# Attention backward for one query row per head: scores as 512-column matmuls in four column groups, spread by one-hot fp32 matmuls

## The chip, the core and the metric

The kernel runs on one core of one Trainium2 chip. The metric is the device time of one execution in microseconds, and the time of a kernel is the median over several executions. A core has a matrix engine (PE, TensorE, with its weight loads listed apart as PEld), a vector engine (DVE), a scalar engine (ACT), a general engine (POOL) and a queue engine (SP). POOL and SP issue the transfers here, and all transfers run on the core's 16 DMA engines.

## The reference

For each of 2 x 32 = 64 heads there is one query row q (128 values), a K and a V of 8192 rows of 128 bf16 values, and a gradient row `grad_out`. The kernel computes the output and the gradients to q, K and V:

```python
scores = jnp.einsum("bhqd,bhkd->bhqk", q, k) * scale     # one row of 8192 a head
p = _softmax(scores, axis=-1)
out = jnp.einsum("bhqk,bhkd->bhqd", p, v)
_out, _vjp = jax.vjp(_f, q, k, v)
_grads = _vjp(grad_out)
```

Written out for a head: s = K q, p = softmax(s x scale), o = p V; dp = V g with g the row of `grad_out`; ds = p (dp - sum(p dp)) x scale; dq = ds K, dK = ds outer q, dV = p outer g. K and V are read once (268 MB together) and dK and dV, of the same size, are written once.

## The kernel before

**Data.** A head's K and its V are tiles of [128 partitions, 64 rows, 128 columns] in bf16, 2 MB each: partition p holds the 64 rows 64p to 64p+63. Twelve such tiles (`NTILE`) are in SBUF, so six heads are under way. A tile is loaded by SP, read by the matrix engine, and then overwritten in place with dK or dV, and stored from there by POOL. The load for the head six later waits for that store (`load`, line 98; `outer`, line 412). In eight heads (`SPREAD`) the dK store is cut in 126 and 2 partitions.

**Chunks and steps.** A tile is worked in four chunks (`NCH`) of 16 rows (`CH`), so a head has eight chunks, first K's, then V's. The loop at line 423 runs over chunks of all heads, and one turn of it is called a step here. The order of all instructions is written out by hand and pinned (`pin`), so each engine works its instructions in just that order. A step holds work of several heads, chosen by r, the step counted from the head's first one. `transpose_chunk` is at r = 0 to 7: 16 transposes of 128 x 128 into PSUM, and one ACT copy of 128 x 2048 to SBUF (`ev`). `score_chunk` follows one step later. `acc` is at r = 8 to 11 for V (o) and 12 to 15 for K (dq). `outer` is at r = 9 to 12 for dV and 13 to 16 for dK. Since a head starts every eight steps, each step has one `transpose_chunk`, one `score_chunk`, one `acc` and one `outer`.

**Scores.** `score_chunk` issues 16 matmuls. Each takes one transposed 128 x 128 block as its weights and the head's q (or g) as its only moving column, so that each gives one column of s or dp, laid out as [128 partitions, 64].

**Sums for o and dq.** `acc` issues four matmuls of 512 moving columns (four rows of the tile side by side). The weights are 64 columns (`CW`) of `E_pad` or `dS_pad`, and the results go to two groups (`NG`) of 64 partitions of one PSUM bank by turns. Only four of the 64 rows of each group's result are wanted, each in one of its four 128-column blocks; `pick` takes them with the mask `diag` (four DVE instructions of 128 x 128), and `join` adds over the partitions by a matmul with ones.

**PSUM.** The transposes have two buffers of two banks, `acc` two banks, the tile `sw` (s, and room for the softmax maximum) one, and `dpw` (dp, the sums, and `qbp`, the broadcast of q or g) one: eight in all.

**The softmax of a head.** `max_part` at r = 4, `max_all` at r = 5, `max_spread` and `expo` at r = 6, `normalise_p` at r = 7, `weigh` at r = 8, `normalise_ds` at r = 9. `broadcast` makes q and g ready in all partitions for `outer`.

Of the kernel before, what the change touches and what calls it, by code (L numbers as in the profile page):

```python
# [11 lines left out]
BF16 = mybir.dt.bfloat16  # L12
F32 = mybir.dt.float32

CH = 16
QT = 4
CW = 64
NG = 2
NTILE = 12
FIRST = 6  # L20
SPREAD = range(4, 60, 7)
# [3 lines left out]
def kernel(  # L25
# [11 lines left out]
    nc = tc.nc  # L37
    B, H, Sq, D = q.shape
    Sk = k.shape[2]
    P = nc.NUM_PARTITIONS  # L40
    assert Sq == 1 and D == P
    BH = B * H
    assert BH <= P
    NT = Sk // P
    assert NT * P == Sk and NT % CH == 0
    NCH = NT // CH
    SL = 2 * NCH
# [4 lines left out]
    pin = tc.keep_in_program_order  # L52

    const = ctx.enter_context(tc.tile_pool(name="const", bufs=1))
    kvp = ctx.enter_context(tc.tile_pool(name="kv", bufs=1))
    evp = ctx.enter_context(tc.tile_pool(name="ev", bufs=2))
    work = ctx.enter_context(tc.tile_pool(name="work", bufs=1))
    small = ctx.enter_context(tc.tile_pool(name="small", bufs=2))
    ps_tp = ctx.enter_context(tc.tile_pool(name="ps_tp", bufs=2, space=bass.MemoryType.PSUM))
    ps_sdp = ctx.enter_context(tc.tile_pool(name="ps_sdp", bufs=1, space=bass.MemoryType.PSUM))  # L60
# [15 lines left out]
    heads = [Head() for _ in range(BH)]  # L76
# [13 lines left out]
    def load(i, w, pieces=(NCH,)):  # L90
        h = heads[i]
        t = kvp.tile([P, NT, D], BF16, tag=f"kv{slot_of(i, w)}", name="kvt")
        h.tile[w] = t
        src = (v_v if w else k_v)[i]
        c = 0
        for m in pieces:
            n0, n1 = c * CH, (c + m) * CH
            pin(load_eng.dma_start(out=t[:, n0:n1, :], in_=src[:, n0:n1, :]))  # L98
            c += m
# [4 lines left out]
    for w, a in enumerate((q, grad_out)):  # L104
        rows = a.rearrange("b h s d -> (b h s) d")
        r0 = FIRST if w == 0 else 0
        if r0:
# [3 lines left out]
                    out=qd_nat[:r0, w, :], in_=rows[:r0], max_dma_last_dim=D  # L111
# [11 lines left out]
    ident_f = const.tile([P, P], F32)  # L123
    masks.make_identity(nc, ident_f[:])
    ones = const.tile([P, 1], F32)
    nc.vector.memset(ones[:], 1.0)
    groups = [g * P // NG for g in range(NG)]
    diag = const.tile([P, QT], F32)
    nc.vector.memset(diag[:], 0.0)
    for g in groups:  # L130
        nc.vector.tensor_copy(out=diag[g : g + CW], in_=ident_f[g : g + CW, g : g + QT])

    NW = NT + CW - QT
    E_pad = const.tile([P, NW], BF16)
# [1 line left out]
    nc.vector.memset(E_pad[:], 0.0)  # L136
    nc.vector.memset(dS_pad[:], 0.0)

    qdT = const.tile([P, 2, BH], BF16)
    for w in range(2):  # L140
        tps = ps_m.tile([P, BH], BF16, tag=f"acc{w}", name="tps")
        nc.tensor.transpose(tps[:], qd_nat[:BH, w, :], ident_bf[:BH, :BH])
        nc.vector.tensor_copy(out=qdT[:, w, :], in_=tps[:])

    dqT = const.tile([P, BH], BF16)
    oT = const.tile([P, BH], BF16)

    def begin_s(i):

        h = heads[i]  # L150
        sw = ps_sdp.tile([P, NT + P + 1], F32, tag="s", name="sw")
        h.s = sw[:, 0:NT]
        h.mT = sw[0:1, NT : NT + P]
        h.mb = sw[:, NT + P :]

    def begin_dp(i):

        h = heads[i]
        dpw = ps_sdp.tile([P, NT + 2 + D], F32, tag="dp", name="dpw")
        h.dp = dpw[:, 0:NT]  # L160
        h.lsum = dpw[:, NT : NT + 2]
        h.qbp = dpw[:, NT + 2 :]

    def broadcast(i, w):

        h = heads[i]
        pin(
            nc.tensor.matmul(  # L168
                h.qbp,
                lhsT=qdT[:, w, i : i + 1].to_broadcast([P, P]),  # L170
                rhs=ident_bf[:],
                start=True,
                stop=True,
            )
        )
        h.qb[w] = small.tile([P, D], BF16, tag=f"qb{w}", name="qb")
        pin(nc.vector.tensor_copy(out=h.qb[w][:], in_=h.qbp))  # L177

    def transpose_chunk(i, c):
        w, c = divmod(c, NCH)  # L180
        src = heads[i].tile[w]
        tp = ps_tp.tile([P, CH, P], BF16, tag="tp", name="tp")
        for t in range(CH):
            pin(nc.tensor.transpose(tp[:, t, :], src[:, c * CH + t, :], ident_bf[:]))  # L184
        ev = evp.tile([P, CH, P], BF16, tag="ev", name="ev")
        pin(nc.scalar.copy(out=ev[:], in_=tp[:]))  # L186
        return ev

    def score_chunk(i, c, ev):
        h = heads[i]  # L190
        w, c = divmod(c, NCH)
        dst = h.dp if w else h.s
        for t in range(CH):
            pin(
                nc.tensor.matmul(  # L195
                    dst[:, c * CH + t : c * CH + t + 1],
                    lhsT=ev[:, t, :],
                    rhs=qdT[:, w, i : i + 1],
                    start=True,
                    stop=True,  # L200
                )
            )

    def max_part(i):
        h = heads[i]
        h.mp = small.tile([P, 1], F32, tag="mp", name="mp")
        pin(nc.vector.reduce_max(out=h.mp[:], in_=h.s, axis=AX.X))  # L207
# [120 lines left out]
    def acc(i, w, c):  # L328
# [6 lines left out]
        for m in range(CH // QT):  # L335
            n0 = c * CH + m * QT
            g = groups[m % NG]
            pin(
                nc.tensor.matmul(  # L339
                    h.acc[w][g : g + CW, :],  # L340
                    lhsT=wts[:, n0 : n0 + CW],
                    rhs=rows[:, n0 : n0 + QT, :].rearrange("p n d -> p (n d)"),
                    start=(c == 0 and m < NG),
                    stop=(c == NCH - 1 and m >= CH // QT - NG),
                )
# [42 lines left out]
    def outer(i, w, c, ends):  # L388

        h = heads[i]  # L390
        n0 = c * CH
        shape = [P, CH, D // 2, 2]
        pin(
            nc.vector.tensor_tensor(  # L394
                out=h.tile[w][:, n0 : n0 + CH, :].rearrange("p n (e t) -> p n e t", t=2),
                in0=h.qb[w][:]
                .rearrange("p (e t) -> p e t", t=2)
                .unsqueeze(1)
                .to_broadcast(shape),
                in1=h.pair[w][:, n0 : n0 + CH, :].unsqueeze(2).to_broadcast(shape),  # L400
                op=ALU.mult,
            )
        )
        if c + 1 in ends:
            at = ends.index(c + 1)
            b0, b1 = (ends[at - 1] if at else 0) * CH, (c + 1) * CH
            dst = (dv_v if w else dk_v)[i]
            if w == 0 and i in SPREAD:
                by_rows(store_eng, dst, h.tile[w], (P - 2, 2))
            else:  # L410
                eng = load_eng if len(ends) > 1 else store_eng
                pin(eng.dma_start(out=dst[:, b0:b1, :], in_=h.tile[w][:, b0:b1, :]))  # L412
# [10 lines left out]
    for g in range(SL * BH + O0 + NCH + 4 - SL):  # L423
        now = [(g // SL - b, g % SL + b * SL) for b in range(4)]
        now = [(i, r) for i, r in now if 0 <= i < BH]

        def at(r0):

            return next((i for i, r in now if r == r0), None)

        def within(r0):

            return next(((i, r - r0) for i, r in now if r0 <= r < r0 + NCH), None)

        if (i := at(O1 + NCH)) is not None and i + AHEAD < BH:
            load(i + AHEAD, 0)
        if (i := at(O0 + NCH)) is not None and i + AHEAD < BH:
            load(i + AHEAD, 1)
        if x := within(O1):
            outer(x[0], 1, x[1], last if x[0] == BH - 1 else whole)  # L440
        if x := within(O0):
            outer(x[0], 0, x[1], last if x[0] == BH - 1 else whole)
        ev = None
        if g < SL * BH:
            i, r = divmod(g, SL)
            if r == 0:
                begin_s(i)
            if r == 3:
                begin_dp(i)
                broadcast(i, 1)  # L450
            if r == 6:
                broadcast(i, 0)
            ev = transpose_chunk(i, r)
        if (i := at(A1 + NCH + 2)) is not None:
            join(i, 1)
        if (i := at(A0 + NCH + 2)) is not None:
            join(i, 0)
        if x := within(A1):
            acc(x[0], 1, x[1])
        if x := within(A0):  # L460
            acc(x[0], 0, x[1])
        if (i := at(NCH + 2)) is not None:
            max_spread(i)
            expo(i)
        if prev is not None:
            score_chunk(*prev)
        prev = (g // SL, g % SL, ev) if ev is not None else None

        if (i := at(NCH)) is not None:
            max_part(i)  # L470
        if (i := at(NCH + 1)) is not None:
            max_all(i)
        if (i := at(NCH + 3)) is not None:
            normalise_p(i)
        if (i := at(SL)) is not None:
            weigh(i)
        if (i := at(SL + 1)) is not None:
            normalise_ds(i)
        if (i := at(A1 + NCH)) is not None:
            pick(i, 1)  # L480
        if (i := at(A0 + NCH)) is not None:
            pick(i, 0)

    for w, (src, dst) in enumerate(((dqT, out_1), (oT, out_0))):
        tps = ps_m.tile([BH, P], BF16, tag=f"acc{w}", name="tps")
# [34 lines left out]
```

## Time and profile before

| what | before |
|---|---|
| median of 8 runs | 1285.68 us (1284.7 to 1289.62) |
| the profiled execution | 1285.78 us, its span 1284.0 us |
| bytes read from and written to HBM | 268.47 MB each |
| busy: PE / PEld / DVE / ACT | 88% / 67% / 73% / 76% |
| DMA queues, share of 16 engines | loads (SP) 49.9%, stores (POOL) 48.8%, instructions 0.7% |

The span is the time from the first to the last instruction of the profiled execution; 1.8 us lie outside it. A busy share is the time in which an engine had an instruction in work. It is an average over the span and doesn't tell what the end waits for. For the DMA engines the page gives, in 40 slices of 32 us, the mean busy share of the 16 engines and the rate in GB/s. The groups of instructions give a kind's count, its busy time in total (overlapping ones counted once), the mean duration of one in ns, and how long the engine stood idle just before them, with what ended the wait.

### The profile page before, as it was taken

What the parts mean: (1) busy time and instruction counts of PE and PEld (TensorE: products, weight loads), DVE (VectorE), ACT (ScalarE), POOL (GpSimd) and SP (SyncE); (2) the same over time, 40 slices, a digit from 0 to 9 for tenths busy, and PEclk for the clock granted to TensorE, in tenths of its full rate; (3) what the DMA queues carried; (4) which work ended last, traced back from release to release, by engine and by line L of the source; (5) the groups of instructions that cost most, each with busy time, mean ns of one, the idle gap of its engine ahead of it and who ended that gap; (6) DMA issues with size and microseconds to landing.
All of it is one profiled execution on the core that took longest, in us unless ns stands there. A gap on an engine that the chain in (4) does not pass through costs nothing.

```text
span 1284.0 us, 42576 instructions
## 1 busy us (share of the span) xinstructions
PE 1129.4 (88%) x19268; PEld 857.8 (67%) x19268; DVE 936.0 (73%) x2122; ACT 975.8 (76%) x641; POOL 76.1 (6%) x143
## 2 busy tenths in 40 slices
PE   6999999989988988898889798997989889889881
PEld 5777777667766766666667576675667667667660
DVE  2888888778777777677777677776778677777772
ACT  6888888878777877787777687886778678777760
POOL 0000000000000000000000000000000000000000
PEclk9999999999999999999999899998989899999895
DMA  9999999999999999999999999999999999999996
GB/s 387 425 427 426 427 426 428 426 428 426 427 428 425 415 428 428 427 420 428 428 427 422 422 429 427 425 426 426 427 426 426 425 427 427 426 424 427 426 410 256
DMA packets 40194, 539.68 MB, mean 420 GB/s; under 512 B 5196, under 2 KB 5196, under 8 KB 6476
## 3 DMA queue, kind: packets, MB, share of 16 engines
q1 hardware_dynamic: 20172, 272.70, 49.9%
q0 software_dynamic: 19840, 264.25, 48.8%
q8 instruction: 150, 2.46, 0.7%
q14 instruction: 32, 0.26, 0.0%
HBM read 268.47 MB, written 268.47 MB: 418 GB/s over the span
## 4 chain that ended last, share of the span: by engine, by line
DMA 31%; another core or an unknown queue 31%; PE 24%; DVE 10%; issue 1%; SPq 1%; ACT 1%; DVEq 0%; ACTq 0%
DMA kvt<-in_v_dram 24%; PE tp L184 10%; PE acc L339 6%; DMA kvt<-in_k_dram 6%; DVE kvt L394 6%; PE dpw L195 3%; PE sw L195 3%; DVE sel L362 2%; SPq L98 1%; ACT ev L186 1%; PE dpw L282 1%; DVE sel L356 1%; DMA qd_nat<-in_q_dram 1%; DVE mp L207 0%
## 5 line engine op out<-in xcount | busy, mean ns | idle before, releaser
L186 ACT COPY ev<-tp 128x2048 bf16<-128x2048 bf16 x512 | 954.9, 1866 | 268.4 <-PE tp L184 257.3
L184 PE MATMUL tp<-ident_bf,kvt 128*128 128x128 bf16 x8192 | 557.4, 223 | 97.3 <-DMA kvt<-in_v_dram 82.3
L394 DVE TENSOR_TENSOR kvt<-qb,pair 128x2048 bf16<-128x2048 bf16 x512 | 621.1, 1214 | 0.2
L184 PEld LDWEIGHTS <-kvt 128*128 128x128 bf16 x8192 | 488.2, 100 | 104.4 <-DMA kvt<-in_v_dram 86.4
L195 PEld LDWEIGHTS <-ev 128*128 128x128 bf16 x8192 | 242.9, 96 | 208.9 <-issue 152.1
L339 PE MATMUL acc<-kvt,dS_pad 128*64 128x512 bf16 x1024 | 169.2, 413 | 0.8 <-DVE dqT L379 0.8
L339 PE MATMUL acc<-kvt,E_pad 128*64 128x512 bf16 x1024 | 160.0, 393 | 0.0
L195 PE MATMUL dpw<-qdT,ev 128*128 128x1 bf16 x4096 | 140.7, 164 | 17.3 <-DVE qb L177 16.5
L362 DVE SCALAR_TENSOR_TENSOR sel<-acc,diag,sel 128x128 f32<-128x128 f32 x384 | 134.6, 351 | 13.6
L195 PE MATMUL sw<-qdT,ev 128*128 128x1 bf16 x4096 | 141.9, 164 | 1.1 <-ACT ev L186 1.1
L207 DVE TENSOR_REDUCE mp<-sw 128x1 f32<-128x64 f32 x64 | 14.4, 225 | 160.4 <-PE sw L195 160.4
L412 POOL DMA_DIRECT2D out_dram<-kvt x118 | 63.4, 537 | 1085.7 <-DVE kvt L394 867.6
L339 PEld LDWEIGHTS <-dS_pad 128*64 128x64 bf16 x1024 | 37.7, 111 | 24.8 <-issue 6.1
L247 DVE CAST E_pad<-E_f 128x64 bf16<-128x64 f32 x64 | 12.5, 195 | 55.8 <-ACT E_f L238 55.8
L339 PEld LDWEIGHTS <-E_pad 128*64 128x64 bf16 x1024 | 36.4, 108 | 21.2 <-issue 0.5
L376 PE MATMUL acc<-ones,sel 128*128 128x1 f32 x256 | 43.5, 239 | 6.2 <-DVE sel L362 6.2
L282 PE MATMUL dpw<-ld,ones 128*128 128x1 f32 x256 | 46.3, 250 | 0.1
L376 PEld LDWEIGHTS acc<-ones,sel 128*128 128x128 f32 x256 | 39.3, 194 | 7.3 <-DVE sel L362 7.3
L356 DVE TENSOR_SCALAR sel<-acc,diag 128x128 f32<-128x128 f32 x128 | 44.1, 345 | 0.0
L253 DVE CUSTOM_DVE_ANT_0 junk<-E_f,dpw 128x64 bf16<-128x64 f32 x64 | 14.1, 221 | 37.5 <-PE dpw L195 37.5
L177 DVE CAST qb<-dpw 128x128 bf16<-128x128 f32 x128 | 35.4, 277 | 6.0 <-PE dpw L168 6.0
L282 PEld LDWEIGHTS dpw<-ld,ones 128*128 128x128 f32 x256 | 38.2, 188 | 0.5 <-DVE ld L253 0.5
(44 smaller groups left out, 314.5 us busy)
## 6 DMA issues: line engine op xcount, KB each, us to landing
out_dram<-kvt POOLq DMA_DIRECT2D x118, 2048.0 KB, 67.8
kvt<-in_v_dram SPq DMA_DIRECT2D x64, 2048.0 KB, 19.8
kvt<-in_k_dram SPq DMA_DIRECT2D x63, 2048.0 KB, 19.9
out_dram<-kvt POOLq DMA_DIRECT2D x8, 2016.0 KB, 73.0
out_dram<-kvt SPq DMA_DIRECT2D x8, 512.0 KB, 22.7
kvt<-in_k_dram SPq DMA_DIRECT2D x2, 512.0 KB, 4.5
kvt<-in_k_dram SPq DMA_DIRECT2D x1, 1024.0 KB, 7.0
out_dram<-kvt POOLq DMA_DIRECT2D x8, 32.0 KB, 72.4
```

The source lines that it names most:

```text
L177: pin(nc.vector.tensor_copy(out=h.qb[w][:], in_=h.qbp))
L184: pin(nc.tensor.transpose(tp[:, t, :], src[:, c * CH + t, :], ident_bf[:]))
L186: pin(nc.scalar.copy(out=ev[:], in_=tp[:]))
L195: nc.tensor.matmul(dst[:, c * CH + t : c * CH + t + 1], lhsT=ev[:, t, :], rhs=qdT[:, w, i : i + 1], start=True, stop=True,)
L207: pin(nc.vector.reduce_max(out=h.mp[:], in_=h.s, axis=AX.X))
L282: nc.tensor.matmul(out, lhsT=ones[:].to_broadcast([P, P]), rhs=col, start=True, stop=True)
L339: nc.tensor.matmul(h.acc[w][g : g + CW, :], lhsT=wts[:, n0 : n0 + CW], rhs=rows[:, n0 : n0 + QT, :].rearrange("p n d -> p (n d)"), start=( ...
L356: nc.vector.tensor_scalar(out=h.sel[:], in0=block, scalar1=diag[:, 0:1], scalar2=None, op0=ALU.mult)
L362: nc.vector.scalar_tensor_tensor(out=h.sel[:], in0=block, scalar=diag[:, b : b + 1], in1=h.sel[:], op0=ALU.mult, op1=ALU.add,)
L376: nc.tensor.matmul(h.acc[w][:, 0:1], lhsT=h.sel[:], rhs=ones[:], start=True, stop=True)
L394: nc.vector.tensor_tensor(out=h.tile[w][:, n0 : n0 + CH, :].rearrange("p n (e t) -> p n e t", t=2), in0=h.qb[w][:] .rearrange("p (e t) -> ...
L412: pin(eng.dma_start(out=dst[:, b0:b1, :], in_=h.tile[w][:, b0:b1, :]))
```

## The change

The scores are made the other way round. The weights are now 32 columns around the head's q, and the moving operand is 512 columns of the transposed chunk. Four such matmuls, one for each group of 32 PSUM partitions, cover a chunk. In `qdT` the q of each head is put at every fourth column, with zeros between them, and the window `q0` is moved back by one column with each chunk. So q stands in the window's column c for chunk c, and chunk c's scores come out in row c of each group; all four chunks add into one bank (`raw`). The rows that belong to other heads' q are not picked.

`keep_raw` copies the bank [128, 512] to SBUF, in fp32, once a half head (K's four chunks, or V's). `spread_rows` then issues four fp32 matmuls, each with a 128 x 128 block of that copy as its weights and the one-hot table `sel4` (16 columns) as the moving operand. They pick the 16 wanted rows and lay the scores out as [128, 64] as before.

s, dp, the sums and `qbp` now share one PSUM tile of one bank (`begin`, at r = 4), and `raw` takes the bank that is left. The steps of the softmax move: `keep_raw` at r = 4 and 8, `spread_rows` at r = 5 and 9, `max_part` from 4 to 5, `max_all` from 5 to 6, `max_spread` and `expo` from 6 to 7, `normalise_p` from 7 to 8, `weigh` from 8 to 9, `normalise_ds` from 9 to 10, and `broadcast` from 3 to 4 for g (it is at 6 for q in both). `transpose_chunk`, `acc`, `outer`, `pick`, `join` and the loads and stores keep their steps. `acc` has the same four matmuls a step, now with 32 weight columns and in four groups of 32 partitions; `diag` and the width of `E_pad` and `dS_pad` follow.

```diff
-CW = 64
-NG = 2
+CW = 32
+NG = 4
+SG = 4
+SW = 32
...
+    sel4 = const.tile([P, NCH, SG], F32)
+    nc.vector.memset(sel4[:], 0.0)
+    for g in range(SG):
+        nc.vector.tensor_copy(
+            out=sel4[g * SW : (g + 1) * SW, :, g],
+            in_=ident_f[g * SW : (g + 1) * SW, g * SW : g * SW + NCH],
+        )
+
+    Q0 = NCH - 1
+    qdT = const.tile([P, 2, Q0 + NCH * BH + SW], BF16)
+    nc.vector.memset(qdT[:], 0.0)
...
+    def begin(i):
+
+        h = heads[i]
+        sw = ps_sdp.tile([P, 2 * NT + 2 * P + 4], F32, tag="s", name="sw")
+        h.score = (sw[:, 0:NT], sw[:, NT : 2 * NT])
+        h.s, h.dp = h.score
+        h.mT = sw[0:1, 2 * NT : 2 * NT + P]
+        h.qbp = sw[:, 2 * NT + P : 2 * NT + 2 * P]
+        h.lsum = sw[:, 2 * NT + 2 * P : 2 * NT + 2 * P + 2]
+        h.mb = sw[:, 2 * NT + 2 * P + 2 : 2 * NT + 2 * P + 3]
...
     def score_chunk(i, c, ev):
+
         h = heads[i]
         w, c = divmod(c, NCH)
-        dst = h.dp if w else h.s
-        for t in range(CH):
+        if c == 0:
+            h.raw = ps_sdp.tile([P, QT * P], F32, tag="raw", name="raw")
+        q0 = Q0 + NCH * i - c
+        for g in range(SG):
             pin(
                 nc.tensor.matmul(
-                    dst[:, c * CH + t : c * CH + t + 1],
-                    lhsT=ev[:, t, :],
-                    rhs=qdT[:, w, i : i + 1],
+                    h.raw[g * SW : (g + 1) * SW, :],
+                    lhsT=qdT[:, w, q0 : q0 + SW],
+                    rhs=ev[:, g * QT : (g + 1) * QT, :].rearrange("p n d -> p (n d)"),
+                    start=(c == 0),
+                    stop=(c == NCH - 1),
+                )
+            )
+
+    def keep_raw(i):
+
+        h = heads[i]
+        h.rows = work.tile([P, QT * P], F32, tag="rows", name="rows")
+        pin(nc.vector.tensor_copy(out=h.rows[:], in_=h.raw[:]))
+
+    def spread_rows(i, w):
+
+        h = heads[i]
+        for t in range(QT):
+            pin(
+                nc.tensor.matmul(
+                    h.score[w].rearrange("p (n t) -> p n t", t=QT)[:, :, t],
+                    lhsT=h.rows[:, t * P : (t + 1) * P],
+                    rhs=sel4[:].rearrange("p c g -> p (c g)"),
                     start=True,
                     stop=True,
                 )
...
-        if (i := at(NCH + 2)) is not None:
+        if (i := at(NCH + 1)) is not None:
+            spread_rows(i, 0)
+        if (i := at(SL + 1)) is not None:
+            spread_rows(i, 1)
+        if (i := at(NCH + 3)) is not None:
             max_spread(i)
             expo(i)
         if prev is not None:
@@ -467,14 +502,18 @@
         prev = (g // SL, g % SL, ev) if ev is not None else None
 
         if (i := at(NCH)) is not None:
+            keep_raw(i)
+        if (i := at(SL)) is not None:
+            keep_raw(i)
+        if (i := at(NCH + 1)) is not None:
             max_part(i)
-        if (i := at(NCH + 1)) is not None:
+        if (i := at(NCH + 2)) is not None:
             max_all(i)
-        if (i := at(NCH + 3)) is not None:
+        if (i := at(NCH + 4)) is not None:
             normalise_p(i)
-        if (i := at(SL)) is not None:
+        if (i := at(SL + 1)) is not None:
             weigh(i)
-        if (i := at(SL + 1)) is not None:
+        if (i := at(SL + 2)) is not None:
             normalise_ds(i)
```

More of the change, by code (lines that the diff above doesn't have):

```diff
@@ L137 @@
     nc.vector.memset(dS_pad[:], 0.0)
-    qdT = const.tile([P, 2, BH], BF16)
+    sel4 = const.tile([P, NCH, SG], F32)
[8 more added lines that the diff above has]
+    nc.vector.memset(qdT[:], 0.0)
     for w in range(2):
@@ L142 @@
         nc.tensor.transpose(tps[:], qd_nat[:BH, w, :], ident_bf[:BH, :BH])
-        nc.vector.tensor_copy(out=qdT[:, w, :], in_=tps[:])
+        nc.vector.tensor_copy(
+            out=qdT[:, w, Q0 : Q0 + NCH * BH].rearrange("p (i f) -> p i f", f=NCH)[:, :, 0],
+            in_=tps[:],
+        )
     dqT = const.tile([P, BH], BF16)
     oT = const.tile([P, BH], BF16)
-    def begin_s(i):
+    def begin(i):
         h = heads[i]
[L151 to L162, printed above, removed]
+        sw = ps_sdp.tile([P, 2 * NT + 2 * P + 4], F32, tag="s", name="sw")
[5 more added lines that the diff above has]
+        h.mb = sw[:, 2 * NT + 2 * P + 2 : 2 * NT + 2 * P + 3]
     def broadcast(i, w):
@@ L169, in broadcast @@
                 h.qbp,
-                lhsT=qdT[:, w, i : i + 1].to_broadcast([P, P]),
+                lhsT=qdT[:, w, Q0 + NCH * i : Q0 + NCH * i + 1].to_broadcast([P, P]),
                 rhs=ident_bf[:],
@@ L191, in score_chunk @@
         w, c = divmod(c, NCH)
-        dst = h.dp if w else h.s
-        for t in range(CH):
+        if c == 0:
+            h.raw = ps_sdp.tile([P, QT * P], F32, tag="raw", name="raw")
+        q0 = Q0 + NCH * i - c
+        for g in range(SG):
             pin(
                 nc.tensor.matmul(
-                    dst[:, c * CH + t : c * CH + t + 1],
-                    lhsT=ev[:, t, :],
-                    rhs=qdT[:, w, i : i + 1],
+                    h.raw[g * SW : (g + 1) * SW, :],
[4 more added lines that the diff above has]
+                )
+            )
+    def keep_raw(i):
[10 more added lines that the diff above has]
+                    rhs=sel4[:].rearrange("p c g -> p (c g)"),
                     start=True,
@@ L445 @@
             i, r = divmod(g, SL)
[L446 to L449, printed above, removed]
+            if r == NCH:
+                begin(i)
                 broadcast(i, 1)
-            if r == 6:
+            if r == NCH + 2:
                 broadcast(i, 0)
```

## The prediction

> **What bounds the kernel now.** I read the page first: engine shares, the DMA slices, the DMA queues.
>
> ```profile
> span 1284.0 us, 42576 instructions
> PE 1129.4 (88%) x19268; PEld 857.8 (67%) x19268; DVE 936.0 (73%) x2122; ACT 975.8 (76%) x641; POOL 76.1 (6%) x143
> ...
> DMA  9999999999999999999999999999999999999996
> GB/s 387 425 427 426 427 426 428 426 428 426 427 428 425 415 428 428 427 420 428 428 427 422 422 429 427 425 426 426 427 426 426 425 427 427 426 424 427 426 410 256
> ...
> q1 hardware_dynamic: 20172, 272.70, 49.9%
> q0 software_dynamic: 19840, 264.25, 48.8%
> q8 instruction: 150, 2.46, 0.7%
> ```
>
> PE looks tight at 88%, but the DMA engines are full in every slice but the last. So the question is whether PE or the DMA engines set the pace, and the waits answer it.
>
> ```profile
> PE tp L184 <- DMA kvt<-in_v_dram: 82.3, 45, 6.1
> PE dpw L195 <- DVE qb L177: 16.5, 51, 0.5
> ```
>
> PE waits 82 us for V loads, and SP's own waits are almost all for a store to free a tile (1139.6 us in 116 waits). Loads wait for stores, compute waits for loads: the DMA engines bound it. How much room has compute? A head moves 4 x 2.097 MB, which at 427 GB/s takes **19.6 us**. In the timeline near 200 us, where loads are still ahead, two stores of the same kind are issued at 200.27 and 217.59: compute needs **17.3 us** a head when nothing holds it up. So there are 2.3 us to spare in each head.
>
> Then the end, in the windows (us, busy time by engine, clock, DMA share, GB/s).
>
> ```profile
> 1180.00:1235.00 55.00, 48.87 (x811) 36.64 (x807) 40.90 (x92) 41.71 (x28) 2.97 (x6) 0.94 1.01 427
> 1240.00:1248.00 8.00, 6.38 (x94) 4.36 (x91) 6.57 (x18) 4.07 (x5) 0.53 (x1) 0.93 0.81 342
> 1248.00:1262.00 14.00, 7.56 (x31) 3.26 (x31) 12.63 (x24) 0.00 (x0) 0.00 (x0) 0.50 1.02 424
> 1264.00:1273.00 9.00, 0.00 (x0) 0.00 (x0) 0.00 (x0) 0.00 (x0) 0.00 (x0) 0.50 0.53 222
> 1273.00:1281.00 8.00, 0.00 (x0) 0.00 (x0) 0.00 (x0) 0.00 (x0) 0.00 (x0) 0.50 0.43 178
> ```
>
> The last compute ends at 1262; transfers go on for 19 us at a share of 0.53 and then 0.43, that is, on 8.5 and then 7 of 16 DMA engines, each at its usual pace (178 / 6.9 = 26 GB/s; 427 / 16 = 27 before). These seven are simply behind the others. As they were full up to 1240 and still have 19 us of work when the last store is given out, I take them to be busy from start to end. Then the end is **the bytes of the late DMA engines over their rate**, and compute may finish up to some 19 us later or any amount earlier without moving it.
>
> **What the Trainium skill says.** "TensorEngine Tiling (Array Packing)", Tiling Modes: 128x32 gives four tiles that work in parallel, and a change of mode drains the engine. The trace shows two tiles: the four `acc` matmuls of a step take 0.55 us, while "TensorE: Matmul & The Clock Gate" (Part 3) gives 2.38 times for three column tiles; no run here shows four yet. "PSUM — Partial Sum Buffer" (PSUM bank collisions): the compiler's scheduler adds a dependency between two engines on one bank and quadrant even where columns differ. The trace agrees: score matmuls waited 16.5 us for the copy of `qbp`, other columns of their bank. "Runtime: NRT & Kernel Launch" (Instruction fetch mechanics): instructions come by the sequencer's own DMA queue in blocks of 16 KiB, 256 instructions. It fits: 2 x 19,268 PE instructions / 256 = 150.5, and queue 8 has 150 packets.
>
> **The change part by part.** All is for one head unless said otherwise.
>
> *Matmuls of the scores.* Out: 128 with one column; a step's 16 take 0.42 us of PE's time (from their start to the next transposes, 216.97 to 217.39). In: 4 a step with 512 columns. Two rounds of two in `acc` take 0.55; a round less, at an estimated 0.216 (512 columns, TensorE page), is 0.34. Bounds: 0.34 if four overlap, 0.55 if only pairs do, 0.86 (4 x 0.216) if none. I take 0.34, as pairs overlap fully in the trace. Eight steps: -0.6 us (from -0.6 to +3.5).
>
> *`acc` in four groups.* 0.55 to 0.34 by the same argument, bounds 0.34 to 0.86: -1.7 us (to +2.5).
>
> *`spread_rows`.* Eight fp32 calls, two instructions each (L282: 256 for 128 calls), whose two weight loads take 0.30 us together (L282, 1243.87 on): +2.4 us; bounds 1.5 (loads overlap) to 2.9 (0.36 each, nothing overlaps). PE's sum is 17.3 - 0.6 - 1.7 + 2.4 = 17.4 us: PE gains nothing, in the likeliest case.
>
> *`keep_raw`.* Two DVE copies of 128x512 fp32 from PSUM. No such row; 64 columns take 225 ns (L207), 128 take 277 (L177), so by that slope 0.59 us, and by 345 for 128 (L356) more: 0.65, bounds 0.59 to 0.8. DVE goes from 936 / 64 = 14.6 to 15.9 us, below 19.6. ACT's copies don't change: 8 x 1.87 + 0.5 = 15.5.
>
> *New waits.* Behind `keep_raw` in DVE's order stand `pick` (0.35 + 3 x 0.35 = 1.45) and the next `outer` (1.21), and only then `max_part`, which reads the one bank that now holds s, dp and `qbp`. The `broadcast` of q opens step 6 on PE and writes that bank, so it waits for `max_part`: 0.65 + 1.45 + 1.21 + 0.23 = 3.5 us after the scores, against 0.98 (transposes) + 0.34 + 1.2 + 0.34 = 2.9 on PE. A stall of 0.6 to 1, with step 6's transposes and ACT's copy behind it. `broadcast` of g at step 4 waits likewise for `normalise_ds`; some 0.3. `spread_rows` needs `keep_raw` and stands a step (1.3 us) behind it: nothing, unless DVE is late. Together about +1, bounds 0 to 2.5. **Compute is then 18.4 us a head** against 19.6: slower than before, still covered. What hides it is the wait for V, which shrinks; with that gone (over 19.6) it costs 64 times the excess.
>
> *Later softmax steps.* `expo` is a step later, but still a step before `acc` reads `E_pad`; the number of steps is the same. In the last head DVE does the closing work; `keep_raw` and the late `E_pad` delay its end by 1 to 2 us, from 1262 to 1264. The 19 us backlog hides that. POOL's and SP's issues keep their order.
>
> *Setup.* A memset of `qdT`, `sel4` and four small copies run on DVE while it waits for q (until 9.6 us): nothing.
>
> *Instructions.* This is the one thing that reaches the DMA engines. Scores: 8192 to 2048 matmuls, spread +1024, so 5120 fewer, each with its weight load: 10,240 instructions of the 38,536, or 40 of the 150 packets. Queue 8 took 0.7% of 16 engines over 1284 us, 9.0 us an engine (0.96 us a packet). So **each DMA engine is relieved of 9.0 x 40/150 = 2.4 us**, if packets are spread evenly. They are whole: an engine has 9 or 10 now and 6 or 7 then, so the last one loses 2 to 4, 1.9 to 3.8 us. If the late engines carried none of them, 0.
>
> Sum against the profiled execution: span 1284.0 - 2.4 = 1281.6; with the 1.8 us outside 1283.4. That execution (1285.78) is 0.1 above the median of 1285.68, so **1283.3 us**, a change of -0.19%. About 0.2% (2.6 us) is what a measurement of this kernel can tell from none, so the sign of a difference is likelier than its verdict.
>
> **Rivals.**
>
> 1. *Compute becomes the bound (slower).* Mechanism: PE's pinned order in which the four column groups don't overlap beyond pairs, or DVE's late `max_part` holds PE at step 6. It decides from 19.6 us a head. With pairs only, PE is 17.4 + 8 x 2 x 0.21 + 1 = 21.8 us: first transposes at 9.6, 64 x 21.8 = 1395, closing work 17, the last store 8: about 1430. With overlap and stalls of 3 us instead of 1, 20.4: about 1340. For: PE is at 98% in the free stretch (176.56 of 180 us, windows), and DVE and PE now wait for each other twice a head. Against: two groups overlap, and 2.3 us are spare. A clock that drops in the longer idle of PE belongs here (near 1217 it was 0.53 after a pause): half speed for some 3 us costs 1.5, inside the spare time. Chance 0.16.
>
> 2. *No gain, or a little later.* The packets of the late engines aren't among those saved, or the later closing work of DVE feeds an engine that had run dry (share 0.81 at 1240 to 1248): 1285 to 1288, chance 0.12. For: the share of 0.81 shows that some engines wait for compute there. Against: those aren't the late ones.
>
> 3. *More gain.* If the late seven carry most of the fetches, 40 packets x 0.96 / 7 = 5.5 us: 1280. For: seven are behind by an equal amount. Against: nothing says which engine fetches. Chance 0.05.
>
> The forecast, 1281.3 to 1285, has the other 0.67. From it come 0.36 faster, 0.27 same and, for the spread between executions, 0.04 slower; the second rival gives 0.02 faster, 0.05 same, 0.05 slower; the third 0.05 faster; the first 0.01 same, 0.15 slower. Altogether 0.43, 0.33 and 0.24. The range leaves out most of the first rival and reaches over the second and third: **1280 to 1290**.
>
> **What would show it.** Right: queue 8 at about 110 packets and 0.5%; DMA share near 1 up to 1235 or so; the tail of some 18 us after the last compute, on about half the engines, still there; PE instructions 14,148; the four `acc` matmuls of a step within 0.4 us; PE still waiting for V. Wrong: if the waits for V vanish, DMA shares fall below 0.97 in the middle slices and PE waits on DVE at L168 or in the spread, compute has become the bound. If the tail after the last compute is gone and the end is no earlier, the late engines weren't busy all along.

## The result, and the profile after

| | before | after |
|---|---|---|
| median | 1286.51 us (56 runs, 1284.7 to 1293.36) | **1282.41 us** (19 runs, 1278.09 to 1286.02) |
| ratio, 95% interval | | **0.9965** [0.9955, 0.9974], or 4.5 us less [3.3 to 5.8] |
| profiled execution, its span | 1285.78, 1284.0 us | 1279.16, 1277.4 us |

The kernel is a little faster. The medians are taken over more runs than those that the prediction saw; they differ by 4.1 us, and the ratio, which has the interval, stands for 4.5. The profiled execution of after is one of its short ones (3.3 us under the median), so its end is read beside a second profile of the same kernel below.

The page of after, engine shares, slices and queues:

```profile
span 1277.4 us, 32475 instructions
PE 1103.9 (86%) x14148; PEld 807.1 (63%) x14148; DVE 1013.5 (79%) x2258; ACT 957.6 (75%) x641; POOL 76.1 (6%) x143
...
DMA  9999999999999999999999999999999999999996
GB/s 388 428 428 427 429 427 430 427 428 428 429 428 428 412 428 428 430 425 428 428 429 427 426 429 428 428 421 428 429 427 425 424 428 430 422 424 428 429 422 273
...
q1 hardware_dynamic: 20172, 272.70, 50.1%
q0 software_dynamic: 19840, 264.25, 49.0%
q8 instruction: 110, 1.80, 0.5%
```

The DMA engines are still full in every slice but the last, the bytes of loads and stores are the same, and queue 8 has 110 packets where it had 150. PE has 5120 matmuls fewer, but its busy time is only 25 us less.

The waits of after:

```profile
PE sw L178 <- DVE mp L240: 70.5, 61, 1.3
...
PE acc L372 <- DVE E_pad L280: 32.0, 58, 1.6
...
PE tp L194 <- DMA kvt<-in_v_dram: 20.6, 13, 3.8
```

The wait for V has fallen from 82.3 to 20.6 us. In its place PE waits for DVE at the broadcast of q, in 61 of 64 heads, and at the first `acc` of V's half, in 58.

The windows of after, the same stretches (us, busy time by engine, clock, DMA share, GB/s):

```profile
1180.00:1235.00 55.00, 46.61 (x616) 34.52 (x612) 44.82 (x101) 41.09 (x27) 3.19 (x6) 0.97 1.01 429
1240.00:1248.00 8.00, 5.05 (x33) 2.69 (x32) 7.79 (x20) 0.00 (x0) 0.53 (x1) 0.60 0.99 419
1248.00:1262.00 14.00, 2.78 (x14) 1.40 (x14) 8.20 (x17) 0.00 (x0) 0.00 (x0) 0.50 0.91 378
1264.00:1273.00 9.00, 0.00 (x0) 0.00 (x0) 0.00 (x0) 0.00 (x0) 0.00 (x0) 0.50 0.47 196
1273.00:1281.00 8.00, 0.00 (x0) 0.00 (x0) 0.00 (x0) 0.00 (x0) 0.00 (x0) 0.60 0.05 19
```

The last compute ends at 1257.5. The tail on about half the engines (0.47) is still there, but from 1273 on it is nearly empty, where before seven engines still worked (0.43). So the time came from the last stretch of the late DMA engines.

Compute has grown tight. From `weigh` of head 3 to that of head 12, where loads are still ahead, a head takes 19.1 us, and 19.3 in heads 15 to 60, where before it took 17.4 and 19.9.

### The profile page after: what moved, and what is told of

The parts are those of the page before. It is cut to its first block, busy times and chain, and to the rows that moved or that the text cites. A ratio compares the mean times of both kernels' runs of the same rounds, so it can differ in the third digit from the quotient of the medians.

```text
span 1277.4 us, 32475 instructions
## 1 busy us (share of the span) xinstructions
PE 1103.9 (86%) x14148; PEld 807.1 (63%) x14148; DVE 1013.5 (79%) x2258; ACT 957.6 (75%) x641; POOL 76.1 (6%) x143
## 4 chain that ended last, share of the span: by engine, by line
DVE 42%; PE 14%; DMA 13%; ACT 10%; another core or an unknown queue 10%; issue 8%; SPq 0%; POOL 0%; ACTq 0%; POOLq 0%; DVEq 0%
DVE kvt L427 23%; DMA kvt<-in_v_dram 10%; ACT ev L196 9%; PE tp L194 8%; DVE sel L395 6%; DVE rows L221 4%; DMA out_dram<-kvt 3%; DVE sel L389 2%; DVE pair L303 2%; PE acc L372 2%; PE raw L208 1%; ACT E_f L271 1%; DVE dSu L349 1%; PE sw L178 1%
## 5 line engine op out<-in xcount | busy, mean ns | idle before, releaser
L194 PE MATMUL tp<-ident_bf,kvt 128*128 128x128 bf16 x8192 | 575.4, 226 | 26.6 <-DMA kvt<-in_v_dram 20.6
L208 PE MATMUL raw<-ev,qdT 128*32 128x512 bf16 x2048 | 211.1, 401 | 5.4 <-ACT ev L196 1.7
L228 PEld LDWEIGHTS sw<-sel,rows 128*128 128x128 f32 x1024 | 124.2, 191 | 29.6 <-issue 13.4
L228 PE MATMUL sw<-sel,rows 128*128 128x16 f32 x1024 | 136.6, 265 | 0.6 <-DVE rl L324 0.6
L372 PE MATMUL acc<-kvt,E_pad 128*32 128x512 bf16 x1024 | 102.9, 391 | 32.0 <-DVE E_pad L280 32.0
L372 PE MATMUL acc<-kvt,dS_pad 128*32 128x512 bf16 x1024 | 112.6, 431 | 0.8 <-DVE dS_pad L358 0.8
L221 DVE COPY rows<-raw 128x512 f32<-128x512 f32 x128 | 87.4, 683 | 20.2 <-PE raw L208 20.0
L178 PE MATMUL sw<-ident_bf,qdT 128*128 128x128 bf16 x128 | 28.5, 223 | 70.6 <-DVE mp L240 70.5
L208 PEld LDWEIGHTS <-qdT 128*32 128x32 bf16 x2048 | 64.9, 95 | 26.7 <-issue 20.2
L315 PEld LDWEIGHTS sw<-ld,ones 128*128 128x128 f32 x256 | 38.2, 188 | 54.5 <-issue 28.4
L315 PE MATMUL sw<-ld,ones 128*128 128x1 f32 x256 | 49.1, 261 | 0.1
## 6 DMA issues: line engine op xcount, KB each, us to landing
kvt<-in_v_dram SPq DMA_DIRECT2D x64, 2048.0 KB, 19.6
```

Source lines behind the costliest of these rows:

```text
L208: nc.tensor.matmul(h.raw[g * SW : (g + 1) * SW, :], lhsT=qdT[:, w, q0 : q0 + SW], rhs=ev[:, g * QT : (g + 1) * QT, :].rearrange("p n d -> ...
L221: pin(nc.vector.tensor_copy(out=h.rows[:], in_=h.raw[:]))
L228: nc.tensor.matmul(h.score[w].rearrange("p (n t) -> p n t", t=QT)[:, :, t], lhsT=h.rows[:, t * P : (t + 1) * P], rhs=sel4[:].rearrange("p ...
L315: nc.tensor.matmul(out, lhsT=ones[:].to_broadcast([P, P]), rhs=col, start=True, stop=True)
L372: nc.tensor.matmul(h.acc[w][g : g + CW, :], lhsT=wts[:, n0 : n0 + CW], rhs=rows[:, n0 : n0 + QT, :].rearrange("p n d -> p (n d)"), start=( ...
```

## The end, engine by engine

The windows show how many DMA engines are busy, not which. The trace also has the time at which each of the 16 parts of a store lands. I use the last store that is issued, and take it that an engine gets to its part when it has worked off all that was queued before. Sorted, the first eight landings of each kernel come within 3.5 us (mostly within 1), and the first of them 2.3 to 5 us after the last compute; the others are behind. The table gives the 10th to 15th landing, "the late six", as their median, and the 16th, in us from the span's start. It has the experiments of the next section too.

| kernel | packets of queue 8 | late six, median (range) | 16th |
|---|---|---|---|
| before | 150 | 1281.4 (1281.2 to 1281.5) | 1282.5 |
| only `acc` in four groups | 150 | 1280.9 (1279.5 to 1282.6) | 1282.7 |
| before with late closing work | 150 | 1281.1 (1279.5 to 1282.2) | 1282.3 |
| after | 110 | 1274.0 (1272.6 to 1275.1) | 1275.9 |
| after, again | 110 | 1274.1 (1273.8 to 1275.2) | 1282.7 |
| after, third | 110 | 1274.2 (1272.8 to 1274.7) | 1275.0 |
| broadcast of q late | 110 | 1274.2 (1273.1 to 1274.8) | 1281.7 |
| only the scores | 110 | 1274.2 (1272.8 to 1275.8) | 1276.7 |
| only the scores, again | 110 | 1274.9 (1272.9 to 1275.4) | 1277.1 |
| only the scores, broadcast late | 110 | 1274.7 (1273.4 to 1278.6) | 1279.2 |
| 24 more packets | 174 | 1285.8 (1285.3 to 1286.5) | 1287.8 |
| 40 more packets | 190 | 1288.6 (1288.2 to 1288.9) | 1291.4 |
| after, ten cut stores | 110 | 1280.0 (1276.1 to 1285.4) | 1287.1 |

Apart from the last row, which adds cut stores, **the late six follow the number of instruction packets and nothing else that was varied**: from 110 to 150 they move by 6.9 us, from 150 to 174 by 4.7, to 190 by 7.5. That is 0.17 to 0.20 us a packet, three times the 0.06 us of an even spread over 16 engines. No run varied the packets apart from the number of PE's instructions, so the table alone doesn't tell the two apart; the packets' own times, next, do.

What does one packet cost in all? I took it from the packets of the trace before. A fetch takes 0.98 us (147.4 us for 150; after, 106.9 for 110). 16-KB packets of stores that run at the same time as a fetch take 632 ns on average, the others 616; of loads, 617 against 613. Summed, that is a loss of **0.37 us** to each fetch. With the fetches' times shifted by 3 us either way the same sum gives -0.03 us, so it isn't an accident of the counting; in after it is 0.35. The loss falls on one packet, the one behind the fetch: in 137 of the 150 cases a data packet that starts within 0.04 us of the fetch's end takes some 1.0 us in place of 0.61, and these packets make up the whole 0.37. A fetch thus costs 1.35 us of DMA engine time, and 40 of them 54 us, or 3.4 us for each of 16 engines if spread evenly. The packet times of all queues, added up and divided by 16, agree: 1277.4 us before, 1273.3, 1274.7 and 1273.1 in the three profiles of after.

But the late six moved by 7 us, not 3.4. So which engines fetch? The trace doesn't name the engine of a packet, but most packets start 3 or 4 ns before another one ends, so that 16 chains can be followed, with some links in doubt. From 600 to 1230 us the parts of one store land over 20 us and more, and a fetch can be put beside the next or last part of a store on its chain. In all profiles but that of experiment 2 there are 850 fetches in that time, and for 658 of them the part's place among the 16 is clear. **542 lie on the seven engines that land 10th to 16th and 72 on the one that lands first**; the eight places in between have 44, which doubtful links may explain. So eight engines carry the fetches or nearly all of them, in about equal shares (542 / 7 = 77), and seven of the eight are the late ones. Each pays 1.35 / 8 = 0.17 us a packet, and for 40 packets 6.8 us, close to the 7 that the late six gained.

The 16th engine is another matter. In two of the four profiles of after and its late-broadcast variant it lands 7 to 9 us behind the six, at 1282, just where the last one landed before. These two profiles are of long executions (1285.85 and 1284.52 us), the others of short ones (1279.16 and 1278.15). So single runs of after go from 1278 to 1288, and the median gains 4.5 us and not 7. Why that engine falls behind isn't shown.

## The experiments

**1. Only `acc` in four groups.**

```diff
 # before
-CW = 64
-NG = 2
+CW = 32
+NG = 4
```

> The kernel before with acc alone in four groups (CW 32, NG 4); scores as before. Theory F (the late DMA engines set the end, so only what they carry counts; the change took instruction packets from them): instruction packets stay at 150, so 0 us against before (within 1 us), though a head's compute without waits falls from 17.3 to about 15.6 us and PE waits longer for V. Theory C (the change gained because PE does less in a step, above all in acc): most of the change's gain is here, 2 to 4 us faster than before. Four acc matmuls of a step: 0.34 us in F and C if four groups overlap, 0.55 if only pairs do.

Measured: 1286.46 us (13 runs), ratio 1.0009 [1.0001, 1.0017]. The four matmuls take 0.33 us from their start to the next instruction instead of 0.55 (0.40 instead of 0.62 to their last end). The row of before and that of this kernel's page (line, operands, count, then busy time and mean ns of one):

```profile
L339 PE MATMUL acc<-kvt,E_pad 128*64 128x512 bf16 x1024 | 160.0, 393 | 0.0
...
L339 PE MATMUL acc<-kvt,E_pad 128*32 128x512 bf16 x1024 | 115.8, 443 | 0.0
```

In the free stretch a head takes 16.0 us (expected 15.6). From 240 us on the granted clock is 0.85, which takes most of that back: PE's busy time falls by 14 us in all, and its wait for V shrinks, from 82.3 to 67.7 us, where it was expected to grow. The time doesn't fall: this half of the change gives nothing.

**2. The same with every score matmul issued twice.**

```diff
 # experiment 1
-        for t in range(CH):
+        for t in [*range(CH), *range(CH)]:
```

> As e1_acc4, and each score matmul issued twice (the same weights, column and result), so 128 matmuls and 128 weight loads a head more: 16,384 instructions, 64 packets of instructions more (214 in all). A head's compute is about 15.6 + 3.4 = 19.0 us, still under 19.6. Theory F: 64 packets x 0.96 us / 16 engines = 3.8 us slower than before and than e1_acc4; if a packet costs as much as the change seemed to gain (4.5 us for 40), 7 us. Theory C: no loss against before as long as compute is covered: within 1 us.

Measured: 1827.47 us, ratio 1.4201 [1.4183, 1.4219]. The page of this kernel, PE's busy tenths and the granted clock in 40 slices:

```profile
PE   7999999999999999999999999999999999999996
PEclk8555555555555555555555555555555555555555
```

PE is busy without a gap and its clock stays at half. A step's 16 transposes take 1.87 us (1.05 before), a head takes 28.2 us, and the DMA share is 0.80, so compute became the bound by its clock. The run says nothing on packets; a smaller dose was needed.

**3. The broadcast of q from step 6 to step 11.**

```diff
 # after
-            if r == NCH + 2:
-                broadcast(i, 0)
...
+        if (i := at(SL + 3)) is not None:
+            broadcast(i, 0)
```

> The changed kernel with the broadcast of q moved from step 6 to step 11 of its head, where nothing on DVE reads its bank, so that PE no longer waits there for max_part (70 us of waits in the changed kernel). A head's compute without waits should fall from 19.8 to about 18.5 us and PE's waits for V come back. Theory F: packets stay at 110, so within 1 us of the changed kernel. Theory C or a mixture (the changed kernel is held up in part by its own compute, 19.8 against 19.6 us): 1 to 4 us faster than the changed kernel.

Measured: 1283.64 us (18 runs), ratio 0.9975 [0.9966, 0.9985]. Waits of this kernel:

```profile
PE sw L178 <- DVE qb L187: 58.7, 62, 1.2
...
PE tp L194 <- DMA kvt<-in_k_dram: 43.0, 30, 2.3
...
PE tp L194 <- DMA kvt<-in_v_dram: 26.3, 21, 4.8
```

The broadcast now waits for a copy and no longer for `max_part`; a head takes 18.0 us in the free stretch instead of 19.1. The saved microsecond comes back as waits for K and V (in after these were 6.0 and 20.6 us), and the time is not shorter. The stall that the change adds costs nothing in the end.

**4 and 11. After, again.** No edit.

> The changed kernel itself beside the others on the same chip. Theory F: 110 packets, 2.4 to 4 us faster than before. Theory C: the same, by its 2 to 4 us; its place against e1_acc4 and e3_q_late tells them apart.

> The kernel after once more, for the direct comparison with the scores part alone and with its late broadcast: 4 to 5 us under before.

Measured: 1281.6 us (8 runs), ratio 0.9966 [0.9952, 0.9979], and 1282.21 us (12 runs), 0.9963 [0.9946, 0.998]. The gain repeats. The profiled execution of the first is a long one (1285.85 us); its last windows are these:

```profile
1264.00:1273.00 9.00, 0.00 (x0) 0.00 (x0) 0.00 (x0) 0.00 (x0) 0.00 (x0) 0.50 0.52 213
1273.00:1281.00 8.00, 0.00 (x0) 0.00 (x0) 0.00 (x0) 0.00 (x0) 0.00 (x0) 0.50 0.09 37
```

A share of 0.09 is 1.4 of 16 engines: from 1274 on one engine is left, which works on to 1282.

**5 and 10. Only the scores: `acc` stays in two groups of 64.**

```diff
 # after
-CW = 32
-NG = 4
+CW = 64
+NG = 2
```

> The changed kernel with acc back in two groups of 64 columns, so the scores' part alone. 110 packets of instructions, as in the changed kernel. Theory F (only what the late DMA engines carry counts, as long as compute is covered): the changed kernel's gain if compute is covered. But acc is back at 0.55 us a step for 0.33, so PE needs up to 8 x 0.2 = 1.6 us a head more, and a head's compute goes from 19.8 to as much as 21.4 us against the transfers' 19.6: then the time is near 64 x 21.4 + 35 = 1405 us at most, and 1300 to 1350 if half of it falls into PE's waits for DVE. Theory C (acc's lighter work is what gained): slower than before by 2 us at most, since scores cost PE nothing more than before.

> The scores part of the change alone (acc stays in two groups of 64), again, beside the kernel after on the same chip. Theory I (instruction packets are the gain): no difference from the kernel after, both about 4 to 5 us under before. If it is below the kernel after by more than the two intervals, the four groups of acc cost something that packets don't show.

Measured: 1279.52 us (4 runs), ratio 0.9947 [0.9929, 0.9965], and 1280.22 us (7 runs), 0.9948 [0.9929, 0.9968]. My fear that compute would bind was wrong. A head takes 19.4 us throughout, and PE is 93% busy at a clock of 0.99. Windows of the first of these runs:

```profile
1180.00:1235.00 55.00, 52.12 (x627) 35.34 (x628) 44.92 (x99) 43.37 (x30) 3.19 (x6) 1.00 0.99 421
1240.00:1248.00 8.00, 7.40 (x92) 5.10 (x89) 6.71 (x13) 6.18 (x4) 0.53 (x1) 1.00 0.87 371
```

Some DMA engines run dry here already (0.99, then 0.87), as compute keeps them waiting, and the last compute ends at 1269.8, 12 us later than in after. It still ends no later, since the late six have their work to 1274 in any case. The scores are the part of the change that gives all of its gain.

**6. 24 more packets: 6 of a step's 16 score matmuls issued twice.**

```diff
 # before
-        for t in range(CH):
+        for t in [*range(CH), *range(6)]:
```

> The kernel before with 6 of the 16 score matmuls of each step issued twice: 48 matmuls and 48 weight loads a head more, 6,144 instructions, 24 packets more (174). PE gets 1.25 us a head more work, 18.6 us of 19.6: covered, if the clock holds. Theory F16 (packets lie on all 16 DMA engines alike): every engine 24 x 0.96 / 16 = 1.4 us later, time +1.4 us. Theory F6 (they lie on the six or so engines that finish late together): these move by 24 x 0.96 / 6 = 3.8 us, from 1280.6 to about 1284.5 in the trace, the early nine stay at 1262.6, and the time is 2.7 to 3.8 us longer. Theory C: 0.

Measured: 1290.2 us (6 runs), ratio 1.0028 [1.0017, 1.004], or +3.6 us [2.2, 5.1]. The even spread (1.4) is excluded, and no effect is too; with the loss of the packet behind, the even spread would give 24 x 1.35 / 16 = 2.0, just below the interval. Over eight engines it is 24 x 1.35 / 8 = 4.1; the late six moved by 4.7. Of this kernel, the queue and two windows:

```profile
q8 instruction: 174, 2.85, 0.8%
...
1273.00:1281.00 8.00, 0.00 (x0) 0.00 (x0) 0.00 (x0) 0.00 (x0) 0.00 (x0) 0.50 0.45 189
1281.00:1289.00 8.00, 0.00 (x0) 0.00 (x0) 0.00 (x0) 0.00 (x0) 0.00 (x0) 0.50 0.25 100
```

The same seven engines (0.45 x 16) work on half through the next window, where before had ended.

**7. Four DVE maxima over 128 x 2048 in the last head, ahead of its first `outer`.**

```diff
 # before, in outer()
+        if i == BH - 1 and w == 1 and c == 0:
+            spare = small.tile([P, 1], F32, tag="mp", name="spare")
+            rows = h.tile[1][:, 0:CH, :].rearrange("p n d -> p (n d)")
+            for _ in range(4):
+                pin(nc.vector.reduce_max(out=spare[:], in_=rows, axis=AX.X))
```

> The kernel before with four maxima over 128 x 2048 (some 2.2 us each) put on DVE before the last head's first outer, so that the closing work and the last eight stores come 8 to 9 us later (last compute at about 1271 in place of 1262). The results of the four are not used. Theory F: the late DMA engines have 18 us of work left at 1262, so the end does not move: within 1 us of before. Rival: the closing work sets the end: 8 to 9 us slower.

Measured: 1286.57 us (13 runs), ratio 1.0001 [0.9992, 1.001]. The last compute moved from 1262 to 1270.6. Windows of this kernel:

```profile
1248.00:1262.00 14.00, 3.04 (x14) 0.96 (x10) 13.76 (x15) 0.00 (x0) 0.00 (x0) 0.50 0.76 323
1264.00:1273.00 9.00, 2.53 (x12) 0.99 (x8) 5.40 (x11) 0.00 (x0) 0.00 (x0) 0.50 0.80 329
1273.00:1281.00 8.00, 0.00 (x0) 0.00 (x0) 0.00 (x0) 0.00 (x0) 0.00 (x0) 0.50 0.41 167
```

Nine engines run dry and are fed later (0.76, then 0.80); the seven others don't notice (0.41, before 0.43). So the early end of compute in after (1257.5) isn't its gain either.

**8. After with two more cut dK stores.**

```diff
 # after
-SPREAD = range(4, 60, 7)
+SPREAD = range(4, 60, 6)
```

> The changed kernel with ten dK stores cut in 126 and 2 partitions in place of eight (SPREAD in steps of 6). In the changed kernel six late engines end near 1273.4, but in its longer executions one engine alone ends near 1282. If that one is among the two that a cut store relieves (1 row for 8), it ends 2 x 7 x 0.61 = 8.5 us earlier and all others 2 x 0.61 = 1.2 us later: the end goes to about 1275 in every execution, the time to 1278 to 1279, 3 us faster than the changed kernel and with less spread. If it is another engine: 1.2 us slower than the changed kernel. Theory C: no difference to the changed kernel.

Measured: 1282.74 us (6 runs), ratio 0.9976 [0.9958, 0.9995]: not better. The late engines are pulled apart instead (1276 to 1287 in the profiled execution, a long one of 1290.24 us). So the 16th engine isn't simply one that such a cut relieves.

**9. 40 more packets: 10 of the 16 issued twice.**

```diff
 # before
-        for t in range(CH):
+        for t in [*range(CH), *range(10)]:
```

> The kernel before with 10 of the 16 score matmuls of a step issued twice, the results unchanged: 5120 more matmuls and weight loads, the mirror image of what the change takes out, so some 190 instruction packets instead of 150. Theory E (fetches fall evenly on 16 engines): 40 x 0.97 / 16 = +2.4 us. Theory U (a packet costs the late engines 0.11 to 0.15 us, as 40 fewer and 24 more have shown so far): +4.4 to +6. Compute is then some 19.1 us a head by the slope of the run with six doubled (17.3 to 18.4), still below 19.6. If the granted clock of TensorE stays near 0.5 instead, as in the run with every one-column matmul twice, compute is the bound, the time is above 1350 and the run says nothing on packets.

Measured: 1295.16 us (10 runs), ratio 1.007 [1.0048, 1.0091], or +9.0 us [6.2, 11.7]; above both figures. Compute took 20.3 us a head in the free stretch, not 19.1, as the granted clock fell to 0.90 between 100 and 200 us; but the DMA engines stayed full, as the windows of this kernel show:

```profile
30.00:100.00 70.00, 69.78 (x1394) 55.20 (x1392) 53.04 (x118) 55.88 (x37) 3.76 (x7) 1.00 1.01 424
100.00:200.00 100.00, 98.30 (x1818) 76.69 (x1816) 69.80 (x157) 72.36 (x48) 6.20 (x11) 0.90 1.01 427
200.00:600.00 400.00, 395.51 (x7881) 312.32 (x7879) 304.46 (x687) 315.08 (x209) 24.50 (x44) 1.00 1.01 424
```

The late six moved by 7.2 us, 0.18 a packet (6.8 expected over eight engines), the mirror image of after. The 16th engine ended another 1.7 us later. All packets of this run, loads and stores too, add up to 7.1 us more an engine than before, of which 40 x 1.35 / 16 = 3.4 are explained; what lengthens the other transfers is open.

**12. Only the scores, with the broadcast of q late.** The edits of experiments 3 and 5 together.

> The scores part alone with the broadcast of q moved from step 6 to step 11, where DVE's max_part is long past. Theory I: the packets are the same 110, so the time is that of the scores part alone, though PE's stall of about 1 us a head before the broadcast is gone. A theory in which compute paces the kernel (19.4 us a head with the stall) expects up to 1 us a head less, some 1.5 to 3 us at the end where the last compute comes earlier.

Measured: 1280.98 us (6 runs), ratio 0.9943 [0.9926, 0.996]. A head still takes 19.4 us, so moving the stall doesn't speed compute up here, and the time is that of the scores alone. These three runs have the lowest ratios of all (0.9943 to 0.9948, after 0.9963 to 0.9966), but the intervals overlap. So it isn't settled whether they beat after by some 2 us or whether only fewer of their executions had the late 16th engine.

## Why the prediction came out right, and where it didn't

The predicted 1283.3 us is 0.9 above the measured median, the range holds it, and the forecast's mechanism is the one that the runs show. But two sums in it are off, and that the number came so close is in part luck.

- **DMA engines bound the kernel; the end is set by the late ones.** Right. Experiments 1, 3 and 7 moved PE's work, its stalls and the last compute, and none moved the end.
- **40 fewer instruction packets.** Right: 110, and 14,148 PE instructions. "Runtime: NRT & Kernel Launch" (Instruction fetch mechanics) calls the cost of a block mostly hidden; whatever holds for PE, it isn't hidden from the DMA engines once these are the bound.
- **"Each DMA engine is relieved of 2.4 us, if packets are spread evenly."** The failing step. The packet's own 0.96 us was about right (106.9 us for 110), but it leaves out the 0.37 us that the packet behind loses, and the spread isn't even: eight engines fetch, so an engine goes from some 19 packets to 14 and not from 9 or 10 to 6 or 7, and the late six gained 7 us. The third rival (5.5 us, late engines carry most fetches) had this mechanism, at a chance of 0.05. I gave it so little because no view of before names the engine that fetches; the chains of its packets do (of 50 fetches with a clear place, 37 on the late seven, 7 on the first). The two errors were covered in part by a thing that I didn't foresee, and this is the luck: an engine that in some executions still lands at 1282 holds part of the gain back. So 2.4 predicted, 7 on the late six, 4.5 in the median.
- **Compute at 18.4 us a head, covered.** Covered it was, but at 19.1 us: 0.5 us below the 19.6 where 1.2 were expected. The timeline of PE in after gives the terms (start, duration, then the group):

```profile
210.05 0.22 PE L178 MATMUL sw<-ident_bf,qdT 128*128 128x128 bf16 x1 [1.25 <-DVE mp L240]
...
214.45 0.40 PE L372 MATMUL acc<-kvt,dS_pad 128*32 128x512 bf16 x4
214.78 0.38 PE L251 MATMUL sw<-gm,ones 1*128 1x1 f32 x2
```

The four matmuls of `acc` take 0.40 us, and 0.33 from their start to the next instruction: predicted 0.34, so four groups do work side by side, as "TensorEngine Tiling (Array Packing)" (Tiling Modes) says. The stall at the broadcast is 1.25 us here and 70.5 / 64 = 1.1 a head, where 0.6 to 1 was expected. The term that I left out is `acc`'s wait for `E_pad`: "still a step before `acc` reads it" was true of the order and not of the time, and it costs 32.0 / 64 = 0.5 us a head.

- **The new operations.** Rows of after (count, then busy time in total and mean ns of one):

```profile
L208 PE MATMUL raw<-ev,qdT 128*32 128x512 bf16 x2048 | 211.1, 401 | 5.4 <-ACT ev L196 1.7
L228 PE MATMUL sw<-sel,rows 128*128 128x16 f32 x1024 | 136.6, 265 | 0.6 <-DVE rl L324 0.6
L221 DVE COPY rows<-raw 128x512 f32<-128x512 f32 x128 | 87.4, 683 | 20.2 <-PE raw L208 20.0
```

The spread takes 136.6 / 64 = 2.1 us a head (predicted 2.4), `keep_raw` 0.68 us (0.65), the scores 211.1 / 512 = 0.41 us a step, of which 0.33 pass before the next instruction (0.34).

- **PE still waits for V.** Hardly: 20.6 us. The list of signs had put this under "wrong", together with a wait of PE at the broadcast, which did come, and a fall of the DMA shares, which didn't (1.01 up to 1235). A wait that shrinks shows that the slack is used up, not that the bound has changed; the share of the DMA engines is the sign that decides.
- **The later closing work.** Predicted 1 to 2 us later and hidden. It ended 4.7 us earlier in the profiled execution and 0.6 later in the long one. It was hidden, as experiment 7 shows for 8 us.

Open: which engine lands 16th, why it is late in some executions only, what makes loads and stores slower in experiment 9, and why just these eight engines fetch.

## What to carry to other kernels

When DMA engines are the bound, count what else they carry: the instruction stream of an engine with many small instructions is part of the load, and fewer, larger matmuls can pay there although the matrix engine itself gains nothing. Read the end engine by engine, since a cost that falls on the engines that end last counts in full, and an average over 16 engines hides it. And before a gain is put down to what looks tight, move that alone: here PE at 88% was not it.

## What the runs showed of the hardware that I had not expected

- A fetch of 16 KB of instructions costs a DMA engine 0.97 us of its own, half as much again as a 16-KB packet of a load or store (0.61 to 0.62 us), and the packet behind it 0.37 us more. In the 13 profiles followed, 614 of 658 fetches lie on eight of the 16 engines, seven of them the late ones, and the late six end 0.17 to 0.20 us later for each packet.
- The granted clock of TensorE doesn't follow from PE's busy share alone. Experiment 2 (32 matmuls of one column beside the 16 transposes of a step, and `acc` in four groups) stayed at 0.50 with PE 99% busy; with 26 of them and `acc` in two groups (experiment 9) it was 0.98 at 96%. `acc` in four groups goes with a lower clock: 0.86 against 0.96 in experiment 1 and before, 0.94 against 0.99 in after and experiment 5; in the second pair PE is also less busy (86% against 93%), and what sets the clock is not shown. "TensorE: Matmul & The Clock Gate" (Part 1) says that the throttled state is the default and that activity releases it; a busy PE in the profile isn't enough for that here.
